# A gated MLP behind block attention on one core: the LayerNorm gain moved from v's rows to the gate, w_sg loaded in natural order, low parts last in batch 0, and a new order

## The chip, the cores and the metric

One core of a Trainium2 chip. Times are device microseconds (us) of one execution; a kernel's time is the median of its runs. Engines are named as the profile names them: PE (TensorE matmuls) and PEld (its weight loads), DVE (VectorE), ACT (ScalarE), POOL (GpSimd), SP (SyncE, which issues nearly all DMAs here).

## The reference, cut to what matters

Eight batches of 576 tokens, 8 heads of 64, all in float32. Attention works in chunks of 64 tokens; its output x (576 x 512 per batch) goes through a gated MLP:

```python
h = x @ w_in                                   # 512 -> 1024
h = 0.5 * h * (1.0 + np.tanh(c * (h + 0.044715 * h ** 3)))
u, v = (h[..., :d_ff // 2], h[..., d_ff // 2:])
mu = np.mean(v, axis=-1, keepdims=True)
var = np.mean((v - mu) ** 2, axis=-1, keepdims=True)
v_n = (v - mu) / np.sqrt(var + 1e-06) * g_ln   # g_ln: one number per feature (512)
v_s = np.einsum('ts,bsd->btd', w_sg, v_n) + b_sg[None, :, None]
gated = u * v_s
return (x + gated @ w_out).astype(np.float32)
```

Since g_ln does not depend on the token, it can be taken out of the sum over s: v_s = g_ln * (w_sg @ v' + b_sg / g_ln), with v' the normalised rows without the gain.

## The kernel before, in words

Every large product runs in pieces: an operand is split into a high part, rounded to the matmul's own format, and a low part (the rest), and three products (high by low, low by high, high by high) are summed in PSUM. `split` does this: ACT copies the high part, DVE subtracts it.

The MLP of a batch has four kinds of step: v units (`v_unit`, 128 tokens each, `m` 0 to 3; unit 4 holds the 64 odd tokens of two batches and runs in even batches only), u products (`u_unit`, `u_fast`), s units (`s_unit`, one per 128 features, which multiply w_sg with v's rows and gate with u) and o products. From batch 2 on (`FAST`) u and o use seven block products in place of eight, which needs sums of blocks (`x_sums`, `w_sums`). Each v unit ends in `normed`: gelu on ACT writes `hs`, DVE takes the statistics (`bn_stats`, `bn_aggr`, an addition), POOL raises to the power -1/2 (`sm<-sm,neg_half`), DVE forms (h - mean) * g (`hs<-hs,sm,g_bc`, with g_ln broadcast over 128 rows in `g_bc`), ACT multiplies by the power and rounds (`v<-hs,sm`), DVE forms the low part (`v<-hs,sm,v`). The bias b_sg enters `s_unit` as extra rows of the last product: rows 64 and 96 of `z2` hold ones, rows 64 and 96 of `wsg_l` the parts of b_sg.

Attention (`att_scores`, `att_transpose`, `att_out`) works on tiles of 128 tokens by 64x64 matmuls. Tiles 0 to 4 (`PE_TILES`) are transposed on PE through one PSUM tile `banks` (`banks<-ident,first_pts`), whose halves also take the tile's output; ACT and DVE carry that output to `xh`, `xl` and `xf`. The weights w_in arrive as 64-bit words; `W` and `w`, `X` and `x` turn them into `win_h`, `win_l` with the help of PE (`ident`, `lows`).

The order of all this is made in two stages. `START` (batches 0 and 1), `SLOTS`, `SUMS` and `ORDER` (batches 2 to 7) list steps: S scores, T transposes, O outputs of a tile, M the load of g_ln, G and g the load and split of w_sg, v, u, s, o as above, Y, V, J parts of weights and sums. Then `Plan` records all operations, and `emit` deals them out to the five engines with a price per operation (`Op.price`), due times counted back from PE's list, and `EARLY`, which shifts the due time of a step. Each engine then runs its list strictly in order. All instructions come out of one line of `emit`, so every row of the profile carries L266 (L271 after the change).

PSUM tiles `pm` and SBUF tiles of the pool `tmp` have four buffers each (`banks` holds one of the four in PSUM while tiles 0 to 4 run).

Of the kernel before, what the change touches and what calls it, by code (L numbers as in the profile page):

```python
# [12 lines left out]
F32 = mybir.dt.float32  # L13
F32R = mybir.dt.float32r
# [11 lines left out]
P = 128  # L26
# [8 lines left out]
LN_EPS = 1e-6  # L35
REST_ODD = ODD // 2
# [12 lines left out]
A0 L0 B0 A1 L1 L2 L3 B1 A2 A3 S0 W0 T0 S1 W1 S2 w0 w1 T1 W2 O0 O1 W3 w2 T2 S3 M0 w3 v00 O2 A4 T3 X0 O3 G0 S4 v01 A8  # L49
T4 O4 B8 x0 X1 v02 X2 x1 v03 X3 U1 v04 g0 x2 g3 x3 U0 g1 P5 F0 g2 u03 g4 u02 s00 P7 T5 F1 T6 s02 s01 Q5 s03 T7 T8 v10  # L50
Y6 Q7 v11 v12 Y3 u10 v13 Y2 u11 Y1 Y0 Y7 u13 Y5 u12 Y4 V0 A12 A10 o01 B10 V1 s10 A11 V2 P9 S13 s11 T9 s12 T10 o02 P11
s13 B11 T13 o00 Q9 T11 o03 A15 T12 o10 O13 V3 B15 B12 o11 Q11 J0 P14 J2 o13 A17 J1 o12
"""

SUMS = {(2, 13): "o3", (2, 8): "o0 o1", (2, 10): "o2"}
# [25 lines left out]
FAST_V = 8  # L81
ORDER = "u0 u1 u2 u3 u4 s0 s1 s2 s3 o0 o1 o2 o3"
# [9 lines left out]
EARLY = {'K*': 1, 'X*': -8, 's03': 2, 'Y0': -2, 'P7': 3, 'v04': -4, 'X0': -1, 'w3': -1, 'W*': -1, 'g4': 4, 'Y7': 2, 'A17': -2, 'x2': -2, 'A12': 1, 'F1': 0, 'B10': 4, 'o02': 2, 'u10': 1, 'T11': 0, 'v13': -1, 'B11': 4, 'u13': 5, 'B12': -2, 'u12': -2, 'u11': 2, 'x3': 2, 'J1': 3, 'P14': -7, 'J0': 0, 's02': -2, 'o10': 0, 'Q7': 4, 'g3': -1, 'Q11': 6, 'u02': 4, 'g0': 2, 'T10': -2, 'S13': -1, 'A10': 3, 'V1': -7, 'T13': -4, 'o01': -1, 'P9': 5, 'P5': -4, 'Q9': -2, 's00': 4, 'B15': 2, 'A11': 1, 'o13': 1, 'V0': -4, 'Q5': 4, 'g2': 8, 'T6': -2, 'Y6': 8, 'g1': -4, 'U0': -2}  # L92
# [44 lines left out]
class Op:  # L137
# [13 lines left out]
    def price(self):  # L151
# [4 lines left out]
        if self.engine == "tensor":  # L156
            x = ins[-1]
            n = outs[0].free_size()
            if x.dtype == F32R:
                return 2.5 + 0.45 * n, 190  # L160
            if x.dtype == BF16:
                return 4.6 + 0.42 * n, 190
            if ins[0].ap[0][1] == D:
                self.quarter = True
                return 29.5, 190
            return (109 if self.method == "transpose" else 1.83 * n + 10), 190
        if self.method == "dma_start" and self.engine == "gpsimd":
            return 1200, DMA_LATE + ins[0].size() / 100
        if self.method == "dma_start":
            row = ins[0].ap[-1][1]  # L170
            return (420 if row >= P else 620), DMA_LATE + ins[0].size() / row / 16 * (5 + 0.16 * row)
# [261 lines left out]
def block_attention_gated_mlp(ctx: ExitStack, tc: tile.TileContext, qkv, w_in, w_out, w_sg, g_ln, b_sg, out):  # L433
# [37 lines left out]
    g_bc = const.tile([P, DH], F32, name="g_bc")  # L471
# [221 lines left out]
    def load_w_sg():  # L693

        st = staged["s"] = [
            mp.tile([P, KT, S], F32, name="stage", tag="u2"),
            tmp.tile([P, S], F32, name="stage", tag="tmp"),
            tmp.tile([P, S], F32, name="bt", tag="tmp"),
        ]
        flat = lambda a: a.rearrange("p (j s) -> p j s", j=2)  # L700
        for j in range(2):
            src = w_sg[:, :4, j * REST_ODD : (j + 1) * REST_ODD]
            nc.sync.dma_start(out=st[0][:, :, j * HS : j * HS + REST_ODD], in_=src)
        for i in range(4):
            nc.sync.dma_start(out=flat(st[0][:, i, :])[:, :, REST_ODD:], in_=flat(w_sg[:, i, ODD:]))
        for dst, src in ((st[1], w_sg[:, 4, :]), (st[2][64:65], b_sg), (st[2][96:97], b_sg)):
            nc.sync.dma_start(out=flat(dst)[:, :, REST_ODD:], in_=flat(src[:, ODD:]))
            nc.sync.dma_start(out=flat(dst)[:, :, :REST_ODD], in_=flat(src[:, :ODD]))

    def split_w_sg(i):  # L710
        nonlocal wsg_h, wsg_l
        st, odd, bt = staged["s"]
        if i == 0:
            wsg_h, wsg_l = (w_sg_tile(i).rearrange("p (i s) -> p i s", i=5) for i in range(2))
            nc.gpsimd.memset(wsg_l[64:128, 4, :].bitcast(F32), 0.0)
        hi, lo = wsg_h[:, i, :], wsg_l[:, i, :]
        if i < 4:
            split(hi, lo, st[:, i, :], nc.scalar, nc.vector)
            return
        nc.scalar.copy(hi, odd)  # L720
        nc.vector.tensor_tensor(lo[0:ODD], odd[0:ODD], hi[0:ODD].bitcast(F32), op=ALU.subtract)

        nc.scalar.copy(lo[64:65], bt[64:65])
        bh = tmp.tile([P, S], F32R, name="bh", tag="tmp")
        nc.scalar.copy(bh[96:97], bt[96:97])
        nc.vector.tensor_tensor(lo[96:97], bt[96:97], bh[96:97].bitcast(F32), op=ALU.subtract)

    def load_misc():
        nc.sync.dma_start(out=g_bc, in_=g_ln.broadcast_to([P, DH]))
# [306 lines left out]
    def v_unit(b, m):  # L1036
# [7 lines left out]
        for kt in range(KT):  # L1044
# [18 lines left out]
    def normed(m, h):  # L1063
# [126 lines left out]
    def s_unit(b, dt):  # L1190
# [12 lines left out]
        nc.vector.tensor_tensor(row, pm[:, :, :HS], row, op=ALU.mult)  # L1203
# [261 lines left out]
```

## Time and profile before

| | us |
|---|---|
| median of 3 runs (lowest, highest) | 494.49 (494.19, 495.76) |
| the profiled execution, its time | 496.37 |
| its span (first to last instruction) | 494.3 |
| PE busy in the span | 473.2 (96%) |
| DVE busy | 400.8 (81%) |
| ACT busy | 335.5 (68%) |
| POOL busy | 126.7 (26%) |
| mean granted PE clock | 0.999 of full |

The busy time of PE counts a matmul from its start to its modelled end, and matmuls overlap, so how fast PE gets on is read from the distance between starts. PE's idle time and the waits behind it are in the list of waits, and the timeline shows at which instruction of a list an engine stood. Idle time of an engine that PE does not wait for costs nothing.

### The profile page before, as it was taken

How to read it: one execution, taken by the hardware profiler on the slowest of the kernel's cores; microseconds unless marked ns; L12 is line 12 of the kernel's file. 1: busy time of each engine (PE TensorE's matmuls, PEld its weight loads, DVE VectorE, ACT ScalarE, POOL GpSimd, SP SyncE). 2: the span in 40 equal slices, each digit the busy share in tenths (PEclk: the TensorE clock that was granted, in tenths of full speed). 3: DMA queues.
4: the chain of work that ended last, by engine and by line, in shares of the span. 5: the costliest groups of instructions: out<-in, count | busy, mean ns of one | idle time of the engine just before them, and what ended most of it. 6: DMA issues, size and time to landing. Idle time of an engine off the chain costs nothing.

```text
span 494.3 us, 12562 instructions
## 1 busy us (share of the span) xinstructions
PE 473.2 (96%) x5076; PEld 433.8 (88%) x5076; DVE 400.8 (81%) x712; ACT 335.5 (68%) x598; POOL 126.7 (26%) x115
## 2 busy tenths in 40 slices
PE   2989999999999999999999989999999999999995
PEld 1557899899999799989999779988999889998995
DVE  7898989887988886989779697888859796777275
ACT  4799698844596998538974698729985396844230
POOL 0105100053424338153203411062301612043000
PEclk9999999999999999999999999999999999999999
DMA  8897100244347525294435443376424703170303
GB/s 316 303 253 186 44 3 23 66 148 135 129 121 208 144 110 158 95 274 123 141 82 183 140 149 97 100 215 181 128 66 120 224 12 127 45 201 25 129 1 95
DMA packets 74746, 65.47 MB, mean 132 GB/s; under 512 B 46397, under 2 KB 59969, under 8 KB 74689
## 3 DMA queue, kind: packets, MB, share of 16 engines
q1 hardware_dynamic: 74416, 64.64, 43.3%
q8 instruction: 40, 0.66, 0.5%
q14 instruction: 18, 0.14, 0.1%
q10 hardware_dynamic: 272, 0.03, 0.0%
HBM read 52.07 MB, written 12.58 MB: 131 GB/s over the span
## 4 chain that ended last, share of the span: by engine, by line
PE 80%; ACT 7%; DVE 5%; DMA 4%; issue 2%; SPq 1%; DVEq 0%; ACTq 0%
PE pm L266 78%; DMA out_dram<-ot 2%; ACT ptT L266 2%; PE banks L266 2%; SPq L266 1%; DMA av<-qkv 1%; DVE nmax L266 1%; DVE ot L266 1%; DMA qk<-qkv 1%; ACT hs L266 1%; DVE wsg L266 1%; ACT v L266 1%; ACT third_pt L266 1%; ACT xf L266 0%; ACT ut L266 0%
## 5 line engine op out<-in xcount | busy, mean ns | idle before, releaser
L266 PE MATMUL pm<-wsg,v 128*128 128x288 f32 x768 | 110.2, 297 | 0.0
L266 PEld LDWEIGHTS pm<-wsg,v 128*128 128x128 f32 x768 | 104.1, 188 | 0.9
L266 ACT COPY ptT<-blocks 32x256 f32<-32x256 f32 (+1 forms) x140 | 62.7, 448 | 5.0 <-DVE blocks L266 1.9
L266 POOL TENSOR_TENSOR sm<-sm,neg_half 128x1 f32<-128x1 f32 x36 | 31.1, 865 | 111.2 <-DVE sm L266 94.4
L266 PE MATMUL pm<-gh,wout 128*128 128x288 f32 x272 | 54.6, 298 | 0.0
L266 PE MATMUL pm<-win_h,xl 128*128 128x512 f32 x128 | 51.5, 403 | 0.6 <-DVE xl L266 0.6
L266 PE MATMUL pm<-win_l,xh 128*128 128x512 f32 x128 | 50.7, 396 | 0.0
L266 PE MATMUL pm<-win_h,xh 128*128 128x512 f32 x128 | 50.5, 395 | 0.0
L266 ACT ACT_TABLE_LOAD x30 | 38.5, 1283 | 15.4 <-DVE pt L266 8.2
L266 PEld LDWEIGHTS pm<-gh,wout 128*128 128x128 f32 x272 | 42.7, 188 | 0.6
L266 POOL TENSOR_TENSOR pt<-pt,nmax 128x512 f32<-128x512 f32 x27 | 30.2, 1129 | 43.8 <-DVE nmax L266 39.7
L266 POOL TENSOR_TENSOR xs<-xf 128x576 f32<-128x576 f32 x12 | 17.2, 1434 | 92.0 <-ACT xf L266 81.2
L266 ACT CAST gh<-u 128x576 fp32r<-128x576 f32 x32 | 21.0, 672 | 27.5 <-DVE u L266 27.2
L266 DVE TENSOR_TENSOR u<-pm,u 128x576 f32<-128x576 f32 x32 | 24.1, 754 | 17.4 <-PE pm L266 16.9
L266 ACT CAST tx<-xs 128x576 fp32r<-128x576 f32 x24 | 16.1, 674 | 29.1 <-POOL xs L266 21.7
L266 PE MATMUL pm<-gl,wout 128*128 128x288 f32 x136 | 34.9, 295 | 0.0
L266 DVE TENSOR_TENSOR ot<-pm,xf 128x576 f32<-128x576 f32 x32 | 24.0, 752 | 10.1 <-PE pm L266 5.5
L266 DVE TENSOR_TENSOR gl<-u,gh 128x576 fp32r<-128x576 f32 x32 | 24.0, 753 | 9.9 <-ACT gh L266 9.8
L266 DVE BATCH_NORM_STATS2 sm<-hs 128x6 f32<-128x512 f32 x36 | 24.6, 685 | 8.7 <-ACT hs L266 8.7
L266 PEld LDWEIGHTS pm<-win_h,xl 128*128 128x128 f32 x128 | 24.0, 188 | 6.4 <-DVE xl L266 1.0
L266 DVE STREAM_TRANSPOSE blocks<-pt 128x512 f32<-128x512 f32 x31 | 21.8, 705 | 9.5 <-POOL pt L266 3.8
L266 PE MATMUL pm<-xh,win_l 128*128 128x288 f32 x112 | 28.5, 301 | 0.8 <-ACT hs L266 0.8
(161 smaller groups left out, 1172.5 us busy)
## 6 DMA issues: line engine op xcount, KB each, us to landing
qk<-qkv SPq DMA_DIRECT2D x31, 512.0 KB, 4.4
out_dram<-ot SPq DMA_DIRECT2D x32, 256.0 KB, 3.1
wx<-kept_u SPq DMA_DIRECT2D x30, 256.0 KB, 3.6
wx<-kept_o SPq DMA_DIRECT2D x30, 256.0 KB, 3.2
av<-qkv SPq DMA_DIRECT2D x116, 64.0 KB, 2.5
wsg<-w_in SPq DMA_DIRECT2D x4, 512.0 KB, 4.4
wout<-w_in SPq DMA_DIRECT2D x4, 512.0 KB, 7.8
st<-w_out SPq DMA_DIRECT2D x8, 256.0 KB, 2.8
```

The lines of the kernel that those rows point to most:

```text
L266: getattr(getattr(self.nc, op.engine), op.method)(*op.args, **op.kwargs)
```

## The change

Six things are changed together.

1. The gain. `normed` no longer multiplies by g_ln: one DVE operation subtracts the mean and multiplies by the power (it now needs POOL's result), ACT only copies the high part, DVE subtracts. `s_unit` multiplies by g_ln in the gate, as a number per partition (`g_col`). In `z2` the rows 64 and 65 hold the parts of 1/g_ln and row 96 its high part; `load_misc` forms them from a 2 KB load: ten small operations, four 128x128 transposes on PE, two copies on ACT. The six memsets of `z2` are gone.
2. w_sg and b_sg come in as they lie in memory (4 DMAs in place of 12) and are put into the order of tokens by `split_w_sg`, whose copies and subtractions go in two pieces each.
3. In batch 0 the products with `win_l` come last in each v unit (`LOW_LAST`).
4. `START`, `SUMS` and `SLOTS` list the steps in another order.
5. `EARLY` has other entries.
6. The prices in `Op.price` differ for DMAs, for 64x64 matmuls and for DVE operations with one wide operand.

```diff
 START = """
-A0 L0 B0 A1 L1 L2 L3 B1 A2 A3 S0 W0 T0 S1 W1 S2 w0 w1 T1 W2 O0 O1 W3 w2 T2 S3 M0 w3 v00 O2 A4 T3 X0 O3 G0 S4 v01 A8
...
+A0 L0 B0 A1 L1 L2 L3 B1 A2 A3 S0 W0 T0 S1 W1 S2 w0 w1 T1 W2 O0 O1 W3 w2 T2 S3 w3 v00 O2 A4 T3 X0 O3 G0 S4 v01 A8 T4
...
 SLOTS = {
-    6: "11:O56 9:T7 1:T5 14:T8 4:S78 14:O78 14:S9A 2:T6",
+    6: "9:T7 2:T5 13:T8 4:S78 14:O78 14:S9A 11:O56 4:T6",
...
+LOW_LAST = (0,)
...
-    for z in z2:
-        zf = z.bitcast(F32)
-        nc.vector.memset(zf[64:128, :], 0.0)
-        nc.vector.memset(zf[64:65, :], 1.0)
-        nc.vector.memset(zf[96:97, :], 1.0)
...
-        for j in range(2):
-            src = w_sg[:, :4, j * REST_ODD : (j + 1) * REST_ODD]
-            nc.sync.dma_start(out=st[0][:, :, j * HS : j * HS + REST_ODD], in_=src)
...
+        for dst, src in (
+            (st[0], w_sg[:, :4, :]), (st[1], w_sg[:, 4, :]), (st[2][64:66], b_sg.broadcast_to([2, S])), (st[2][96:97], b_sg)
+        ):
+            nc.sync.dma_start(out=dst, in_=src)
...
+        by_halves(nc.scalar.copy, hi, src)
+        minus = lambda a, x, y: nc.vector.tensor_tensor(a, x, y.bitcast(F32), op=ALU.subtract)
+        by_halves(minus, lo[:n], src[:n], hi[:n])
...
     def load_misc():
-        nc.sync.dma_start(out=g_bc, in_=g_ln.broadcast_to([P, DH]))
+        nc.sync.dma_start(out=g_col, in_=g_ln.rearrange("o (k p) -> p (o k)", p=P))
...
+        for k in range(KT):
+            nc.tensor.transpose(ps[:, k * P : (k + 1) * P], rows[:, k, :], ident)
+        for z in z2:
+            nc.scalar.copy(z[64:128, :], ps[64:128, :])
...
+        if b in LOW_LAST:
+            steps.sort(key=lambda x: x[1].tensor.name == win_l.tensor.name)
...
-        nc.vector.scalar_tensor_tensor(h, h, mv[:, 0:1], g_bc, op0=ALU.subtract, op1=ALU.mult)
+        nc.vector.tensor_scalar(h, h, mv[:, 0:1], rs, op0=ALU.subtract, op1=ALU.mult)
...
-            nc.scalar.mul(hi, h, rs)
-            nc.vector.scalar_tensor_tensor(lo, h, rs, hi.bitcast(F32), op0=ALU.mult, op1=ALU.subtract)
+            split(hi, lo, h, nc.scalar, nc.vector)
...
-        nc.vector.tensor_tensor(row, pm[:, :, :HS], row, op=ALU.mult)
+        nc.vector.scalar_tensor_tensor(row, pm[:, :, :HS], g_col[:, dt : dt + 1], row, op0=ALU.mult, op1=ALU.mult)
```

Three places show how the engines' lists move. The first is PE's list from the second tile's transposes to the first v unit (`pm<-win_h,xl`). In the rows, `banks<-...first_ptT` are outputs of a tile, `pm<-qkv_w` and `pm<-qkv_u` scores of tiles 2 and 4 and of tile 3, `ident` and `lows` the weights' conversion. Before:

```order
L266 MATMUL pm<-win_l,ident 128x512
L266 MATMUL banks<-first_ptT,av 64x64 x16
L266 MATMUL pm<-qkv_w 64x64 x16
L266 MATMUL pm<-wsg_97,ident 128x512
...
L266 MATMUL banks<-ident,third_pt 128x128 x4
L266 MATMUL pm<-win_h,xl 128x512
...
L266 MATMUL pm<-win_l,xh 128x512
L266 MATMUL pm<-win_h,xh 128x512
...
L266 MATMUL banks<-first_ptT,qkv_w 64x64 x16
L266 MATMUL pm<-qkv_w 64x64 x16
L266 MATMUL pm<-wsg_110,ident 128x512
```

After:

```order
L271 MATMUL pm<-qkv_w 64x64 x16
L271 MATMUL banks<-first_ptT,av 64x64
L271 MATMUL pm<-win_l,ident 128x512
L271 MATMUL pm<-wsg_97,ident 128x512
L271 MATMUL banks<-first_ptT,av 64x64
...
L271 MATMUL pm<-qkv_w 64x64 x16
L271 MATMUL banks<-ident,third_pt 128x128 x4
L271 MATMUL pm<-win_h,xl 128x512
L271 MATMUL pm<-win_h,xh 128x512
...
L271 MATMUL pm<-win_l,xh 128x512 x4
L271 MATMUL banks<-first_ptT,qkv_w 64x64 x16
L271 MATMUL pm<-wsg_110,ident 128x512
```

Scores of tiles 2, 3 and 4 moved ahead, the outputs of tile 0 and the scores of tile 3 are now cut up by conversions, and the four products with `win_l` stand at the end of the unit.

The second is ACT's list in the v units of batch 6 (`hs<-pm` is the gelu that empties a v unit's PSUM tile; `z` and `v` are high parts, `ptT<-blocks` a tile's transposed probabilities). Before:

```order
L266 ACT_TABLE_LOAD
L266 ACTIVATE hs<-pm 128x512 x2
L266 CAST tx_572<-xs 128x576
L266 ACTIVATE v<-hs,sm 128x512
L266 COPY ptT<-blocks 128x512
L266 COPY ptT<-blocks 32x8x32
L266 ACTIVATE hs<-pm 128x512
L266 COPY ptT<-blocks 32x8x32 x3
L266 ACTIVATE hs<-pm 128x512
...
L266 COPY ptT<-blocks 32x8x32
L266 ACTIVATE hs<-pm 128x512
```

After:

```order
L271 ACT_TABLE_LOAD
L271 ACTIVATE hs<-pm 128x512 x2
L271 COPY xf<-xf_ident 128x4x32
L271 COPY xf<-xf_lows 128x4x32
L271 ACTIVATE hs<-pm 128x512
...
L271 COPY ptT<-blocks 32x8x32 x2
L271 ACTIVATE hs<-pm 128x512
L271 CAST v<-hs 128x512
L271 COPY ptT<-blocks 32x8x32 x2
L271 ACTIVATE hs<-pm 128x512
```

The third gelu now stands ahead of the first high parts, and the fourth and fifth follow sooner.

The third is DVE's list at the end of the v units of batch 7. Before:

```order
L266 TENSOR_SCALAR sm<-sm 128x1
L266 SCALAR_TENSOR_TENSOR v<-hs,sm,v 128x512
L266 SCALAR_TENSOR_TENSOR hs<-hs,sm,g_bc 128x512
L266 BN_STATS sm<-hs 128x6
L266 SCALAR_TENSOR_TENSOR v<-hs,sm,v 128x512
L266 BN_AGGR sm<-sm 128x2
L266 TENSOR_SCALAR sm<-sm 128x1
L266 SCALAR_TENSOR_TENSOR hs<-hs,sm,g_bc 128x512
L266 SCALAR_TENSOR_TENSOR v<-hs,sm,v 128x512
```

After:

```order
L271 TENSOR_SCALAR hs<-hs,sm 128x512
L271 BN_STATS sm<-hs 128x6
L271 BN_AGGR sm<-sm 128x2
L271 TENSOR_TENSOR v<-hs,v 128x512
L271 TENSOR_SCALAR sm<-sm 128x1
L271 TENSOR_SCALAR hs<-hs,sm 128x512
L271 TENSOR_TENSOR ut<-pm,ut 128x576
L271 TENSOR_TENSOR v<-hs,v 128x512
```

The wide operation on `hs` stood directly behind the addition before, where POOL's power ran beside it; it now needs that power, and in this last unit it still stands directly behind the addition.

## Rows read from the trace of the kernel before

**Rows 1.** The page: span, and the busy line of its part 1.
```profile
span 494.3 us, 12562 instructions
...
PE 473.2 (96%) x5076; PEld 433.8 (88%) x5076; DVE 400.8 (81%) x712; ACT 335.5 (68%) x598; POOL 126.7 (26%) x115
```

**Rows 2.** Waits of PE: us in total, times, longest.
```profile
PE pm L266 <- DMA qk<-qkv: 7.2, 2, 4.3
PE pm L266 <- ACT hs L266: 2.3, 2, 1.5
PE banks L266 <- ACT first_pts L266: 2.3, 1, 2.3
PE banks L266 <- DVE xl L266: 1.3, 1, 1.3
PE pm L266 <- ACT ut L266: 0.7, 2, 0.5
...
PE pm L266 <- DVE xl L266: 0.6, 1, 0.6
```

**Rows 3.** Timeline of PE, 34 to 38: start, us, instruction, [idle before].
```profile
34.76 0.66 PE L266 MATMUL banks<-ident,first_pts 128*128 128x128 f32 x4 [1.29 <-DVE xl L266]
35.17 0.48 PE L266 MATMUL pm<-win_h,xl 128*128 128x512 f32 x1
...
35.95 0.39 PE L266 MATMUL pm<-win_h,xl 128*128 128x512 f32 x1
36.27 1.15 PE L266 MATMUL banks<-first_ptT,qkv_u 64*64 64x64 f32 x32
37.35 0.51 PE L266 MATMUL pm<-win_l,xh 128*128 128x512 f32 x1
37.69 0.40 PE L266 MATMUL pm<-win_h,xh 128*128 128x512 f32 x1
37.93 0.40 PE L266 MATMUL pm<-win_h,xl 128*128 128x512 f32 x1
```

**Rows 4.** Timeline of ACT at 30.
```profile
30.18 1.28 ACT L266 ACT_TABLE_LOAD   x1
```

**Rows 5.** Timeline of ACT in batch 6, 397 to 403.
```profile
397.25 0.60 ACT L266 ACTIVATE hs<-pm 128x512 f32<-128x512 f32 x1 [0.22 <-DVE v L266]
...
399.13 0.60 ACT L266 ACTIVATE hs<-pm 128x512 f32<-128x512 f32 x1
...
402.94 0.60 ACT L266 ACTIVATE hs<-pm 128x512 f32<-128x512 f32 x1
```

**Rows 6.** Groups on DVE: out<-in, shapes, count, then busy us, mean ns, idle before.
```profile
L266 DVE SCALAR_TENSOR_TENSOR hs<-hs,sm,g_bc 128x512 f32<-128x512 f32 x36 | 27.6, 773 | 0.0
L266 DVE TENSOR_TENSOR u<-pm,u 128x576 f32<-128x576 f32 x32 | 24.1, 754 | 17.4 <-PE pm L266 16.9 <-ACT u L266 0.4
L266 DVE SCALAR_TENSOR_TENSOR v<-hs,sm,v 128x512 fp32r<-128x512 f32 x32 | 23.8, 749 | 4.4 <-ACT v L266 4.1
...
L266 DVE TENSOR_TENSOR pt<-pt,nmax 128x512 f32<-128x512 f32 x4 | 2.6, 679 | 0.1
...
L266 DVE TENSOR_SCALAR wsg<-wsg 128x512 f32<-128x512 f32 x4 | 1.7, 417 | 0.0
```

**Rows 7.** Groups on ACT: the high part with and without a factor.
```profile
L266 ACT ACTIVATE v<-hs,sm 128x512 fp32r<-128x512 f32 x32 | 22.9, 723 | 7.4 <-POOL sm L266 3.1 <-DVE hs L266 2.9 <-DVE sm L266 1.1
...
L266 ACT CAST wx<-r 128x512 fp32r<-128x512 f32 x6 | 3.4, 619 | 1.9 <-DVE wout L266 1.8
```

**Rows 8.** Groups on POOL.
```profile
L266 POOL TENSOR_TENSOR sm<-sm,neg_half 128x1 f32<-128x1 f32 x36 | 31.1, 865 | 111.2 <-DVE sm L266 94.4 <-ACT wout L266 8.4 <-ACT hs L266 3.6
...
L266 POOL TENSOR_TENSOR xs<-xf,xs 128x576 f32<-128x576 f32 x12 | 19.5, 1629 | 29.2 <-DVE tx L266 28.1 <-DVE nmax L266 1.1
```

**Rows 9.** Timelines of DVE and POOL at 13: two operations beside each other.
```profile
13.37 1.53 DVE L266 TENSOR_TENSOR win_l<-wsg,win_h 128x512 fp32r<-128x512 f32 x1
...
13.05 1.30 POOL L266 TENSOR_TENSOR first_pts<-first_pts,nmax 128x512 f32<-128x512 f32 x1 [11.74 <-DVE nmax L266]
```

More of the change, by code (lines that the diff above doesn't have):

```diff
@@ L35 @@
 LN_EPS = 1e-6
+G_TINY, G_TOP = 1e-30, 3.0e38
 REST_ODD = ODD // 2
@@ L170, in price @@
             row = ins[0].ap[-1][1]
-            return (420 if row >= P else 620), DMA_LATE + ins[0].size() / row / 16 * (5 + 0.16 * row)
+            each = 15 + 0.22 * min(max(row - 64, 0), 192) + 0.09 * max(row - 256, 0)
+            return (420 if row >= P else 620), DMA_LATE + ins[0].size() / row / 16 * each
         wide = [a for a in ins if a.free_size() > 1]
@@ L186, in price @@
                 return (170 if self.method == "reciprocal" else 100 if self.method == "bn_aggr" else 70), 85
-            one = len(ins) == 1 and not psum and self.method in ("tensor_copy", "tensor_scalar")
+            one = len(wide) == 1 and not psum and self.method in ("tensor_copy", "tensor_scalar")
             three = self.method == "scalar_tensor_tensor" and not psum and len(ins) > 2
@@ L470, in block_attention_gated_mlp @@
     win_l = const.tile([P, KT, DF], F32R, name="win_l")
-    g_bc = const.tile([P, DH], F32, name="g_bc")
+    g_col = const.tile([P, KT], F32, name="g_col")
     neg_half = const.tile([P, 1], F32, name="neg_half")
@@ L716, in split_w_sg @@
         hi, lo = wsg_h[:, i, :], wsg_l[:, i, :]
+        src, n = (st[:, i, :], P) if i < 4 else (odd, ODD)
+        by_halves(nc.scalar.copy, hi, src)
+        minus = lambda a, x, y: nc.vector.tensor_tensor(a, x, y.bitcast(F32), op=ALU.subtract)
+        by_halves(minus, lo[:n], src[:n], hi[:n])
         if i < 4:
-            split(hi, lo, st[:, i, :], nc.scalar, nc.vector)
             return
-        nc.scalar.copy(hi, odd)
-        nc.vector.tensor_tensor(lo[0:ODD], odd[0:ODD], hi[0:ODD].bitcast(F32), op=ALU.subtract)
-        nc.scalar.copy(lo[64:65], bt[64:65])
+        by_halves(nc.scalar.copy, lo[64:66], bt[64:66])
         bh = tmp.tile([P, S], F32R, name="bh", tag="tmp")
-        nc.scalar.copy(bh[96:97], bt[96:97])
-        nc.vector.tensor_tensor(lo[96:97], bt[96:97], bh[96:97].bitcast(F32), op=ALU.subtract)
+        by_halves(nc.scalar.copy, bh[96:97], bt[96:97])
+        by_halves(minus, lo[96:97], bt[96:97], bh[96:97])
     def load_misc():
-        nc.sync.dma_start(out=g_bc, in_=g_ln.broadcast_to([P, DH]))
+        nc.sync.dma_start(out=g_col, in_=g_ln.rearrange("o (k p) -> p (o k)", p=P))
+        gain = tmp.tile([P, S], F32, name="gain", tag="tmp")
+        rows = gain[:, : 4 * P].rearrange("p (k c) -> p k c", k=KT)
+        part = [gain[:, 4 * P + i * KT : 4 * P + (i + 1) * KT] for i in range(3)]
+        nc.gpsimd.memset(gain, 0.0)
+        nc.scalar.activation(part[0], g_col, AF.Abs)
+        nc.vector.tensor_scalar(part[0], part[0], G_TINY, G_TOP, op0=ALU.max, op1=ALU.min)
+        bits = g_col.bitcast(I32)
+        nc.vector.scalar_tensor_tensor(
+            bits, bits, -0x80000000, part[0].bitcast(I32), op0=ALU.bitwise_and, op1=ALU.bitwise_or
+        )
+        nc.vector.reciprocal(part[0], g_col)
+        hi = part[1].bitcast(F32R)
+        split(hi, part[2], part[0], nc.scalar, nc.vector)
+        for at, src in ((64, part[1]), (65, part[2]), (96, part[1])):
+            nc.vector.tensor_copy(rows[:, :, at : at + 1], src.unsqueeze(2))
+        ps = ps_m.tile([P, 2, 512], F32, name="pm")[:, 0]
+        for k in range(KT):
+            nc.tensor.transpose(ps[:, k * P : (k + 1) * P], rows[:, k, :], ident)
+        for z in z2:
+            nc.scalar.copy(z[64:128, :], ps[64:128, :])
     wout_h = wout_l = wsg_h = wsg_l = None
```

26 lines of the change are left out of this document (11 added, 15 removed), and 8 rows, old and new, of the table SLOTS.

## The prediction

> **What bounds the kernel now.** I read the page first: PE is busy in 473.2 of a span of 494.3 us, DVE in 400.8, ACT in 335.5 [rows 1]. So PE sets the end, and what can be won is its idle time, 494.3 - 473.2 = 21.1 us. The list of PE's waits says what that is made of [rows 2]: 7.2 us for the first tiles' data, which the change does not touch (the first 11 DMAs stand in the same order); 2.3 for the second tile's softmax; then 1.3 and 0.6 on the low parts `xl`, 2.3 on gelus of v units, 0.7 on copies `ut`. The waits behind the first two tiles add up to 1.3 + 0.6 + 2.3 + 0.7 = 4.9 us; most of the rest is the empty end behind the last matmul, whose list is the same after the change. Whatever DVE and ACT save, the kernel gains at most about 5 us, and only where one of these waits ends sooner. The timeline then shows where two of them sit: PE stands 1.29 us before the transposes of tile 3 at 34.76 [rows 3], and in batch 6 the fifth gelu of the v units comes 3.8 us behind the fourth (402.94 against 399.13) [rows 5].
>
> **The change, part by part.**
>
> *Off DVE and ACT.* The wide operation on `hs` takes 773 ns 36 times [rows 6]. It becomes a `TENSOR_SCALAR` with two operands per partition. No row has that form; the nearest one, the same operation on 128x512 floats with constants, takes 417 ns, and the ceiling is that nothing changes, 773. I take 417, since only the source of the two numbers differs: 36 x 0.356 = 12.8 us of DVE. The Trainium skill, "VectorE: DVE Perf Modes", section "Mode 2×_2P — use both read ports for one tensor", says that an operation with one tensor of float32 in SBUF can deliver two elements per cycle and one with two tensors cannot; by it the 417 would hold, and were it void here the saving would be 0. The low part goes from 749 to a subtraction as at 679: 32 x 0.07 = 2.2 us off. The gate has a third operand now; 754 is the floor, and I put the same 0.07 on top, 32 x 0.07 = 2.2 us added. DVE loses about 13 us net. On ACT the high part falls from 723 to 619 ns [rows 7], 3.3 us over 32, and its list has 28 table loads in place of 30, each 1.28 us [rows 4]. None of this is on PE's path by itself.
>
> *On PE, added.* Four transposes for 1/g_ln. Four like them took from 34.76 to 35.17, 0.41 us [rows 3]; they stand between u products in a stretch where PE doesn't wait: +0.4 us. Their PSUM tile is held until two copies on ACT are done, and I cost that at nothing, since some forty u products follow them in the list; without that cover it is two copies at 0.62.
>
> *On PE, detours.* Going from large to 64x64 matmuls and back costs time: 36.27 - 35.95 = 0.32 us into one, and 37.69 - 37.35 = 0.34 behind it, against 0.24 between neighbours (37.93 - 37.69) [rows 3], so about 0.2 us for a round trip. I counted 75 changes of size in PE's list before and 85 after: five more round trips. One of them stands late, +0.2. Four stand in the first 35 us, where PE partly waits anyway: 0 to +0.8, I take +0.4.
>
> *The early stage.* The scores of tile 4 come before v00, so ACT does both exponentials ahead of one table load instead of loading three times between 30 and 40 us. This takes two loads, 2.56 us, from ACT where it is nearly full. The low parts last in v00 let it start without `win_l` of the last block. Against it: tile 3's transposes now have only one conversion between them and tile 2's output, where before the scores of tile 4 stood there too, and they still need the `xl` that DVE forms from that output behind a statistics operation. So the 1.29 us can shrink or grow. Ends: all of it goes (-1.3, and -1.1 more if half of the 2.3 of the second tile went too) or nothing does (0). I take -0.9, nearer to the first end, since the two table loads that go are worth twice the wait.
>
> *The late waits.* In batch 6 the third gelu moves ahead of the first high parts and the others follow it; the five gelus lose about four operations of 0.6 us ahead of the last one. The shorter of the two gelu waits, 2.3 - 1.5 = 0.8 us [rows 2], goes: -0.8. The longer, in batch 4, has the same gelus behind the same neighbours, each 0.1 shorter; it begins with a store that lands late, which stays: -0.3 of 1.5. The `ut` waits (0.7) lie behind high parts and table loads that get shorter or go: -0.4. The `xl` wait in batch 1 has one shorter copy ahead of it: -0.2 of 0.6.
>
> *DMAs.* SP issues 8 fewer, and one broadcast of 256 KB gives way to a load of 2 KB in single elements. No row has such a load. It stands before the loads of two u weight blocks, which wait for their buffers anyway; I take 0, between a gain of half a microsecond and a loss of one.
>
> **Sum:** 0.4 + 0.2 + 0.4 - 0.9 - 0.8 - 0.3 - 0.4 - 0.2 = -1.6 us, against the profiled execution's 496.37 (span 494.3 and 2.07 around it): 494.8. That execution lies 1.9 above the median of the runs; carried to the median of 494.49 it gives **492.9 us**, faster by 0.32%. About 0.3%, 1.5 us, is what a measurement of this kernel can tell from no change (its own three runs span 0.3%), so the forecast lies just beyond that line.
>
> **The rivals.**
>
> *The waits move, nothing is won.* DVE has no slack in the first 50 us, and its list puts the softmax of tile 4 ahead of the `xl` of tile 2's output. Then tile 3's transposes wait as long as before while conversions that stood ahead of them are still to do: the early -0.9 becomes +0.3. Of the late waits only batch 6's goes, -0.8. With 0.4 + 0.2 + 0.4 this gives +0.5: 495.0, no measurable change. For it: PE's list shows two conversions behind the transposes that stood ahead before. Against it: ACT's two table loads.
>
> *DVE stands at the gain.* In `normed` the wide operation needs POOL's power now, where it ran beside it before. The power takes 865 ns, and an `xs` ahead of it on POOL 1629 [rows 8]. DVE runs in order, so behind a waiting `hs` stand the low parts and the additions to `ut` that free PSUM. A second way to the same: DVE and POOL hinder each other. At 13 us a subtraction took 1.53 us beside a POOL multiplication of 1.30 [rows 9], against 0.68 for its kind [rows 6]. The Trainium skill, "SBUF — State Buffer", section "Who interferes with whom", speaks of a port pair that one of the two holds for a whole instruction, the fast one-tensor operation included; the trace agrees for two-tensor operations, with the 1.53. It decides if DVE stands more than the 0.43 us per unit that it saves; per batch of four units a microsecond each is 4 - 1.7 = 2.3 us late. If in each of the six batches from the third on PE then waits once more for the 0.5 us of the longest `ut` wait [rows 2], that is +3.0, with 1.0 added and the early -0.9: 494.49 + 3.1 = 497.6, slower. Against it: DVE's list mostly has two to four other operations between the addition and `hs` (only the last unit of batch 7 has none), and PE has 72 u products to do before it needs v.
>
> *All waits go.* With DVE 13 us lighter, the 4.9 us vanish and only 0.6 (transposes and the late round trip) is added: 490.2.
>
> **How the numbers follow.** Forecast as summed, with small errors either way, faster: 0.40; all waits gone or nearly so: 0.12; together faster 0.52. No measurable change: 0.34. DVE stands at the gain, slower: 0.14. The range reaches from the third case, with the other 1.1 us of the early bound, 490.2 - 1.1 = 489.1, up to 494.49 + 1.4 = 495.9, where nothing is won and all is added (0.4 + 0.2 + 0.8). The slow rival lies outside, 0.14. The forecast's own range is 491.0 to 493.0.
>
> **What would show it.** Right: 36 `TENSOR_SCALAR` on `hs` near 0.42 us, DVE at about 388 us busy, PE's wait on `banks` for `xl` under 0.7, one gelu wait left in PE's list, near 1.2 us, and PE idle in about 20 us or less. The early term is wrong if the first products with `wsg` and v's rows start no sooner than before. The slow rival shows as DVE waiting for `sm` from POOL, some microseconds per batch, with PE waiting for `ut` or for v's low parts. If DVE and ACT are lighter as said, PE's waits are as long as before and the time stays, the second case holds.

## The result, and the profile after

The changed kernel takes 498.48 us (median of 6 runs, 496.58 to 498.9), the kernel before 494.5 in the same set: a ratio of 1.0068, 95% interval 1.0048 to 1.0088. A second set, with more runs of before, gives 498.44 against 495.61, 1.0050 (1.0036 to 1.0063). So it is slower, by the ratios 2.5 to 3.4 us, where 1.6 us less was forecast.

Its profiled execution is the fastest of its eleven (496.58); the page therefore looks like that of before [rows 1], span and busy PE alike:

```profile
span 494.4 us, 12537 instructions
...
PE 472.9 (96%) x5076; PEld 433.3 (88%) x5080; DVE 395.4 (80%) x719; ACT 331.1 (67%) x607; POOL 119.8 (24%) x116
...
L271 POOL TENSOR_TENSOR sm<-sm,neg_half 128x1 f32<-128x1 f32 x36 | 24.3, 674 | 104.3 <-DVE sm L271 104.2
...
L271 ACT ACT_TABLE_LOAD x28 | 35.9, 1283 | 8.6 <-DVE pt L271 4.0
```

DVE is 5.4 us lighter, not 13; ACT has its two table loads less. The groups that answer to rows 6 and 7 (DVE, then ACT; count, then busy us, mean ns, idle before):

```profile
L271 DVE SCALAR_TENSOR_TENSOR u<-pm,g_col,u 128x576 f32<-128x576 f32 x32 | 26.0, 813 | 19.7 <-PE pm L271 19.5
L271 DVE TENSOR_TENSOR v<-hs,v 128x512 fp32r<-128x512 f32 x32 | 23.2, 730 | 2.8 <-ACT v L271 2.5
L271 DVE TENSOR_SCALAR hs<-hs,sm 128x512 f32<-128x512 f32 x36 | 19.4, 540 | 0.9 <-POOL sm L271 0.7
...
L271 ACT CAST v<-hs 128x512 fp32r<-128x512 f32 x32 | 19.6, 619 | 7.2 <-DVE hs L271 6.8
```

The operation on `hs` takes 540 ns, between the 417 I took and the 773 of before; the last column answers the slow rival, since DVE stood for POOL's power only 0.7 us in all. All 36 took 498 to 550 ns, with POOL at work beside them or not, so POOL is not what lengthens them; of the 36 of before, one that ran beside POOL's multiplication `r` took 1.78 us, and the mean of the others is 744. The Trainium skill, "VectorE: DVE Perf Modes", section "Mode 2×_2P — use both read ports for one tensor", makes the one-tensor form the faster one: the 540 against 773 agrees in direction, but the form with two operands per partition did not reach the 417 of the form with constants.

The list of PE's waits is where the change shows [rows 2]:

```profile
PE pm L271 <- DMA qk<-qkv: 7.3, 3, 4.3
PE banks L271 <- ACT first_pts L271: 2.6, 1, 2.6
PE banks L271 <- DVE xl L271: 1.3, 2, 0.8
PE pm L271 <- DVE wsg L271: 0.8, 1, 0.8
PE pm L271 <- ACT first_ptT L271: 0.6, 1, 0.6
PE pm L271 <- ACT ut L271: 0.6, 2, 0.4
PE pm L271 <- DVE gain L271: 0.5, 1, 0.5
PE pm L271 <- DMA av<-qkv: 0.5, 2, 0.3
PE pm L271 <- DVE ot L271: 0.5, 1, 0.5
PE pm L271 <- DVE xl L271: 0.5, 1, 0.5
PE pm L271 <- DVE ut L271: 0.4, 1, 0.4
```

The gelus (`hs`, 2.3 before) are gone from it, both of them, where the prediction had one left near 1.2. In their place stand shorter waits that before did not have: for `wsg` (ahead of a conversion at 32.64), `gain`, `av`, `ot`, for DVE's `ut`, and a second place on `xl`. (The 0.6 for `first_ptT` is no new one: it lies at 13.5, where before waits 0.6 for `wsg`.)

To see where the time went in every trace, I cut PE's timeline at five products that all kernels have: A ends at the first product of the third v unit, B at batch 1's first v unit, C at the 137th `pm<-gh,wout` (in batch 2), D and E at the first v unit of batches 4 and 5, F at the last `pm<-gh,wout`. "rise" is the time at which the trace's record of TensorE's clock begins, at 2.4 GHz.

```
kernel          rise     A      B      C      D      E      F    falls of the clock
before          18.96  39.91  43.25  121.37  67.47  53.06  157.30
before_again    17.93  39.61  43.25  121.40  68.28  50.87  157.96
before_again2   19.33  39.85  43.25  121.40  68.08  52.63  157.34
changed         16.49  40.19  44.37  123.03  68.29  50.63  155.91
a_again         19.87  41.76  44.39  123.69  68.32  50.45  156.05
b_gain          18.75  39.50  44.93  122.09  68.69  52.03  157.30
b_newprice      17.08  41.59  44.04  121.98  68.46  52.28  156.46
b_neworder2     19.80  39.91  43.93  123.08  70.14  53.96  159.67   at 300
b_listprice     18.48  42.21  43.89  122.95  69.88  51.89  156.64
a_oldorder      17.25  40.49  44.95  122.01  67.98  50.61  156.64
a_oldprice      17.94  39.60  48.04  121.64  69.31  52.41  158.23   at 62
a_rowgain       18.30  41.06  43.92  124.43  68.68  50.96  156.56
o_rowgain       19.39  41.72  44.53  121.87  68.74  50.59  157.32
a_early         19.57  44.08  44.37  123.31  68.31  50.47  156.58   at 37
a_early_row     18.56  44.87  44.44  123.53  68.97  51.17  156.14   at 36
o_early         19.64  44.09  44.09  122.19  67.95  50.70  156.12   at 37
o_early_row     20.01  44.05  45.74  122.37  68.04  50.68  156.30   at 37
a_early24       19.02  41.41  44.39  122.92  68.30  50.07  156.42
a_early42       19.19  40.06  46.17  123.23  68.39  50.13  156.02
o_early24       17.25  40.69  44.08  122.31  68.34  50.33  156.95
```

The changed kernel (two traces) against before (three): A +0.3 to +2.2, B +1.1, C +1.6 to +2.3, E -0.2 to -2.6, F -1.3 to -2.1. It loses in about the first 210 us (A to C) what it wins in batches 4 to 7, and more.

### The profile page after: what moved, and what is told of

Read it like the earlier page. It is cut to its first block, busy times and chain, and to the rows that moved or that the text cites. A ratio compares the mean times of both kernels' runs of the same rounds, so it can differ in the third digit from the quotient of the medians.

```text
span 494.4 us, 12537 instructions
## 1 busy us (share of the span) xinstructions
PE 472.9 (96%) x5076; PEld 433.3 (88%) x5080; DVE 395.4 (80%) x719; ACT 331.1 (67%) x607; POOL 119.8 (24%) x116
## 4 chain that ended last, share of the span: by engine, by line
PE 63%; DVE 13%; ACT 10%; DMA 7%; SPq 3%; issue 2%; ACTq 0%; DVEq 0%
PE pm L271 62%; SPq L271 3%; ACT ptT L271 3%; DMA qk<-qkv 2%; DMA out_dram<-ot 2%; DVE sm L271 2%; DMA wout<-w_in 2%; ACT L271 1%; DVE ot L271 1%; DVE v L271 1%; DMA av<-qkv 1%; DVE nmax L271 1%; DVE xl L271 1%; PE banks L271 1%; ACT hs L271 1%
## 5 line engine op out<-in xcount | busy, mean ns | idle before, releaser
L271 POOL TENSOR_TENSOR sm<-sm,neg_half 128x1 f32<-128x1 f32 x36 | 24.3, 674 | 104.3 <-DVE sm L271 104.2
L271 PE MATMUL pm<-win_l,xh 128*128 128x512 f32 x128 | 48.4, 394 | 0.0
L271 DVE SCALAR_TENSOR_TENSOR u<-pm,g_col,u 128x576 f32<-128x576 f32 x32 | 26.0, 813 | 19.7 <-PE pm L271 19.5
L271 DVE TENSOR_REDUCE nmax<-pm 128x16 f32<-128x1024 f32 (+1 forms) x22 | 22.5, 1022 | 9.3 <-PE pm L271 9.2
L271 PEld LDWEIGHTS pm<-win_h,xh 128*128 128x128 f32 x128 | 24.0, 188 | 5.2
L271 PEld LDWEIGHTS pm<-win_l,xh 128*128 128x128 f32 x128 | 24.0, 188 | 5.1
```

The costliest lines, as they stand in the source:

```text
L271: getattr(getattr(self.nc, op.engine), op.method)(*op.args, **op.kwargs)
```

## The experiments

Each ratio is to the kernel before, on the same chip in the same set, with its 95% interval; medians of before by set are 495.61, 494.67, 496.39, 495.34 and 496.13.

**The changed kernel again, and before twice more.** No edit.

> The changed kernel, unaltered, a second time. Its profiled execution had a span of 494.4 us, five other executions 496.1 to 496.8, and the kernel before has 494.3 in its profile but a median of 494.5 in time, so the trace at hand is not the usual case. Theory A (the loss lies in a stage whose timing varies from execution to execution): the new trace has a span near 496.3, and beside the first one it shows 2 us more in one place, most likely in the first 50 us. Theory B (every execution of the changed kernel carries the loss in the same waits, and only the first trace was lucky): the time is 498.5 again, and the 2 us are spread over many waits of 0.3 to 0.8 us. Expected: median 498.0 to 498.9.

Measured: 498.44 us. The new trace (span 496.7) is 1.57 us behind the first one at the end of A and 0.66 in C, and nowhere else by more than 0.2. So both theories hold in part: most of the spread comes from the first 20 us (PE's rows are 1.57 us apart from there to 40 us, one by one), the rest from waits in batch 2.

> The kernel before, unaltered, a second time. Its profiled execution (496.37) lies above the median of its runs (494.5 to 495.6 in three sets). Theory luck (the waits that the prediction meant to remove, 1.7 us at 286 and 0.95 at 402, belong to that execution and are the 1.9 us by which it exceeds the median): this trace has a span of 492 to 493.5 and lacks one or both waits. Rival (they stand in every execution, and the spread comes from the moment at which the clock rises): both waits are there again within 0.2 us, and the 40-us milestone moves with the rise by 0.46 us per us, as it does between five traces of the changed early order.

> The same once more, for a third trace: of three, theory luck expects the two waits in one or at most two; the rival expects them in all.

Measured: 495.72 (0.9984, 0.9968 to 0.9999: the same kernel twice, so 0.16% is what chance does) and 496.54 in one run. The wait for gelus in PE's list is 2.3 us in the first trace [rows 2], 2.0 in the third, but 0.7 in the second, whose E is 50.87: the wait in batch 4 stands in two of three, that of batch 6 in all. So 1.5 of the 2.3 us that the prediction saw there stand in two executions of three, and not in the third. Stage A hardly moves with the rise here.

**Parts of the change, each alone or left out.** Names with a_ are made from the changed kernel, with b_ from the kernel before, with o_ from the changed kernel with the lists of before. b_gain is before with the gain at the gate; b_newprice with the three prices; b_neworder2 with the four lists (M0, the load of g_ln, stays where before has it, since there the first v unit still needs g_bc); b_listprice with both; a_oldorder and a_oldprice are the changed kernel with the lists, or the prices, of before. For example:

```diff
-            return (420 if row >= P else 620), DMA_LATE + ins[0].size() / row / 16 * (5 + 0.16 * row)
+            each = 15 + 0.22 * min(max(row - 64, 0), 192) + 0.09 * max(row - 256, 0)
+            return (420 if row >= P else 620), DMA_LATE + ins[0].size() / row / 16 * each
```

> The changed kernel with the four lists of the kernel before; only M0 stands where the changed kernel has it, before g0. Theory order: 493 to 495, since DVE and ACT are lighter and the old lists have their few waits. Theory gain: 497.5 to 498.5, as the changed kernel. If lists and edits only work together: above 499.

> The kernel before with the gain moved to the gate and 1/g_ln in z2 (M0 before g0), its own lists, prices, load of w_sg and order of products in batch 0. Theory order: 493 to 495. Theory gain: 497 to 498.5, and the trace shows PE waiting for gain (0.5 us) and, in most batches, for v's low parts or for ut.

> The changed kernel with the three prices of the kernel before; lists, gain, w_sg and order of products as changed. PE's list up to the first v unit is again that of the kernel before. Theory early (the new prices pulled scores and conversions of weights ahead, to where a matmul still takes twice as long, and cost about 1.4 us by 40 us): the milestone at 40 us (first product of the third v unit) stands 1 to 1.5 us sooner than in the changed kernel at the same moment of the clock's rise, and the time is 496.5 to 497.5. Rival (the early stage differs only by the moment at which the clock rises, which is chance): 498.4 as the changed kernel.

> The kernel before with the changed kernel's three prices and nothing else. Its PE list up to the first v unit is that of the changed kernel. Theory early: slower than before by 1 to 2 us, 496.5 to 497.5. Rival (chance of the clock alone): 495 to 496, no change.

> The kernel before with the changed kernel's four lists alone (M0, the load of the gain, stays where the kernel before has it). Theory order (the new lists put PE in front of sums, copies and outputs that are late in batches 2 and 3): 497 to 499, with new waits of 0.5 to 0.9 us on ut and ot between 150 and 270 us, and without the 1.7 us wait at 286. Theory gain and early only: 494 to 495.5, since in the changed kernel's trace batches 4 and 6 gain 3.7 us against the trace of before.

> The kernel before with both the changed kernel's lists and its prices, but with its own gain in v's rows, load of w_sg and order of products. Lists alone gave +1.6%, prices alone +0.7%. Theory fit (lists and prices belong together and were each useless alone): within 0.3% of before or faster, 493.5 to 496. Theory sum (each costs by itself): +2% or more, above 502. Between them (496.5 to 500): the lists fit the gain at the gate too.

Measured:

| kernel | us | ratio |
|---|---|---|
| a_oldorder | 496.42 | 1.0015 (1.0002 to 1.0028) |
| b_gain | 499.80 | 1.0085 (1.0068 to 1.0103) |
| b_newprice | 498.59 | 1.0073 (1.0053 to 1.0093) |
| b_neworder2 | 502.21 | 1.0159 (1.0132 to 1.0186) |
| b_listprice | 502.15 | 1.0122 (1.0099 to 1.0145) |
| a_oldprice | 503.73 | 1.0169 (1.0143 to 1.0195) |

No theory explains this alone, and the parts do not add up. Each costs 0.7 to 1.6% by itself, lists and prices together 1.2% where their sum is 2.3%, and the whole 0.5 to 0.7%. One can be left out with profit, the lists: a_oldorder takes 496.42, the changed kernel in the same set 498.44, 1.0015 (1.0002 to 1.0028) against 1.0050 (1.0036 to 1.0063), two intervals that do not meet. So with gain and prices in place the new lists cost 2.0 us, and the 0.15% that is left is hardly more than chance. That a part alone leaves the planner with lists tuned for something else would fit the other results, but no run shows it. The load of w_sg and the low parts last are in every a_ and o_ kernel and were never run alone, so what they are worth is open.

The stages tell the parts apart. *Prices*: PE's rows up to the first product of the first v unit go with the prices (the kernels with the new ones share one order there, those with the old ones another), and A goes with them: 39.5 to 39.9 with the old, 40.2 to 42.2 with the new. b_newprice and b_listprice, which lack the low parts last, lie 1.1 us above the line of the changed kernel's A against the rise (given below); this fits a gain by the low parts. *Gain*: B is 43.25 before, 43.9 to 44.0 in the kernels that changed only lists or prices, and 44.4 to 45.0 with the transposes (48.0 in a_oldprice is taken up below), so 0.6 to 0.8 of the growth needs no transposes. b_gain shows in small what its theory asked for: a wait of 0.48 for `gain`, and in each of batches 2 to 6 one of 0.27 to 0.63 for `ut` or v's low parts. *Lists*: C is 121.4 to 122.1 with the old lists, 123.0 to 123.7 with the new ones in four traces of five (a_oldprice has 121.6). *Batch 4*: but for one execution of before, an E of 51 or less came only with gain and new prices together (b_gain 52.0, b_newprice 52.3, b_listprice 51.9).

Two of these kernels show something more. In a_oldprice the clock fell. PE's timeline there, and behind it the busy time by stretch (us, PE busy, granted clock, DMA share, GB/s):

```profile
60.37 0.63 PE L270 MATMUL pm<-ident,gain 128*128 128x128 f32 x4 [0.98 <-DVE gain L270]
62.15 0.73 PE L270 MATMUL pm<-xh,win_l 128*128 128x288 f32 x2 [1.15 <-ACT z L270]
62.68 0.68 PE L270 MATMUL pm<-xl,win_h 128*128 128x288 f32 x2
63.16 0.68 PE L270 MATMUL pm<-xh,win_h 128*128 128x288 f32 x2
```

```profile
58.00:62.00 4.00, 2.02 (x71) 1.00 0.41 131
62.00:66.00 4.00, 3.85 (x17) 0.57 0.00 0
66.00:70.00 4.00, 4.00 (x33) 1.00 0.02 4
```

After waits of 0.98 and 1.15 us, with 64 products of 64x64 ahead of the first and four transposes between them, the granted clock is 0.57 over four microseconds, the level of 1.2 GHz for most of them, and a pair of products advances by 0.48 us (62.68 to 63.16), against 0.26 to 0.27 in the changed kernel's timeline at 61. In b_neworder2 one wait of 2.08 us did the same:

```profile
298.20 0.40 PE L266 MATMUL pm<-xh,wx 128*128 128x288 f32 x1 [2.08 <-ACT ut L266]
```

So a wait of two microseconds can cost more than its own length. It need not: o_early_row (below) waits 2.32 us at 75.44, and the clock stays up.

```profile
74.00:78.00 4.00, 2.56 (x74) 1.00 0.02 3
78.00:82.00 4.00, 4.00 (x33) 1.00 0.01 4
```

The Trainium skill, "TensorE: Matmul & The Clock Gate", section "HAM oscillation — how this bites in real kernels", names idle gaps of PE as what lets the clock fall, and longer ones than these. The traces agree in the kind and not in the length: 2.08 us was enough in one execution, 2.32 was not in another.

**1/g_ln without PE.** a_rowgain writes the parts to DRAM and reads them back as rows; o_rowgain is the same with the lists of before.

```diff
-        for k in range(KT):
-            nc.tensor.transpose(ps[:, k * P : (k + 1) * P], rows[:, k, :], ident)
-        for z in z2:
-            nc.scalar.copy(z[64:128, :], ps[64:128, :])
+        for i in range(2):
+            nc.sync.dma_start(out=rows[i : i + 1, :].rearrange("o (k p) -> p (o k)", p=P), in_=part[1 + i])
+        for z in z2:
+            nc.sync.dma_start(out=z[64:66, :].bitcast(F32), in_=rows)
+            nc.sync.dma_start(out=z[96:97, :].bitcast(F32), in_=rows[0:1, :])
```

> The changed kernel with 1/g_ln brought into z2's rows by DMA (parts written to DRAM, read back as rows) in place of four transposes on PE, and M0 moved ahead of w3. Theory gain on PE: the transposes and PE's wait for them cost 1.1 us (a step of 0.93 us before them, 0.43 for them), so the milestone at 83 us stands 1.0 to 1.3 us sooner and the time is 497.0 to 497.5. Rival (the stretch up to 83 us is bound by DVE and ACT, and PE waits elsewhere as long): 498.0 to 498.9.

> The changed kernel with the four lists of before, M0 where before has it, and 1/g_ln brought into z2's rows by DMA instead of four transposes. With the old lists and the transposes it was 1.0015 of before, with 1.4 us of PE's time lost ahead of the transposes and 0.43 in them. Theory gain on PE: 1.0 to 1.7 us less than that, 0.997 to 0.999 of before, which beats both kernels. Rival (any edit of the plan shifts waits elsewhere by a us or more): 1.001 to 1.008.

Measured: 499.88 (1.0095, 1.0074 to 1.0117) and 498.49 (1.0050, 1.0033 to 1.0068). B is 43.92 and 44.53, so 0.4 to 0.5 us come back there, and nothing of it reaches the end: both are slower than the kernels that they were made from. o_rowgain lies in the range of its rival; a_rowgain lies above the ranges of its theory and of its rival (which ended at 498.9), with PE waiting elsewhere: 1.05 for `xl` at 93.48, where the changed kernel waits 0.48, and a C of 124.43.

**The first 30 us alone, the rest kept row by row.** The planner deals the operations out twice, the second time with the DMA price of before; whatever starts before the cut in the second plan comes first, in that order. a_early cuts at 30 us, o_early does so with the lists of before; the `_row` kernels also leave out the transposes.

```diff
+        at2 = None
+        for _ in range(3):
+            at2 = self.run(users, after, at2)
+        at = [b - 1e6 if b < FIRST else a for a, b in zip(at, at2)]
```

> The changed kernel, its order behind the first v unit kept instruction by instruction; only the first 30 us are dealt out with the DMA price of before, so that the four conversions of weights stand again behind the 64x64 products. Theory early: the 40-us milestone stands at -0.4 to 0 us against the first trace of before, whatever the moment of the clock's rise (the changed kernel: +0.3 to +1.85, 0.46 us per us of later rise), and the gain is kept to the end: 1.0 to 1.4 us under the changed kernel, a ratio of 1.002 to 1.004. Rival (what is won early is lost at the next wait on DVE, as with the transposes): ratio 1.005 to 1.007 as before.

> As a_early, and the four transposes and two copies for 1/g_ln taken out of the lists (six DMAs bring the rows to z2), everything else in its place. Theory: PE gets on 0.7 to 1.1 us further by 83 us, ratio 1.000 to 1.002. Rival: PE waits for xl at 91 us that much longer, ratio as a_early.

> The changed kernel with the four lists of before (1.0015 of before), and the first 30 us as in a_early, everything else in its place. Theory: 1.0 to 1.4 us under that, ratio 0.9985 to 0.9997. Rival: 1.0015 again.

> As o_early, without the transposes and copies for 1/g_ln. Theory: 0.7 to 1.5 us less than o_early, ratio 0.9955 to 0.998, which beats both kernels. Rival: as o_early.

Measured: 500.41 (1.0100, 1.0077 to 1.0122), 501.91 (1.0121, 1.0092 to 1.0149), 498.90 (1.0069, 1.0048 to 1.0090) and 501.99 (1.0151, 1.0116 to 1.0185). All miss. The cut itself made a wait, and the clock fell behind it (a_early):

```profile
35.20 1.12 PE L280 MATMUL pm<-wsg,ident 128*128 128x512 f32 x2 [3.20 <-DVE wsg L280]
```

The rows by DMA came too late for the first products with `z`; o_early_row stood there for 2.32 us:

```profile
75.44 0.76 PE L286 MATMUL pm<-wsg,z 128*128 128x288 f32 x4 [2.32 <-DMA z<-rows]
```

**The cut moved to 24 and to 42 us.**

> As a_early, with the cut at 24 us instead of 30: a_early stood 3.4 us at 31.5, where the work of the two pieces met badly, and its clock fell to 1.2 GHz behind that wait. PE's first 30 rows are those of before, the other engines' lists differ from the changed kernel's in 15 to 19 rows. Theory early: the first product of the first v unit stands within 0.5 us of before's (the changed kernel: +1.2 to +2.8), the 40-us milestone at 0 to +0.5 whatever the rise, and the time 0.5 to 1.4 us under the changed kernel, ratio 1.002 to 1.005. Rival (the wait ahead of the weights' conversion at 32 us takes it all): the 40-us milestone at +1 or more, ratio 1.005 to 1.007.

> The same with the cut at 42 us: the whole early stage, tile 3 and the first three v units in the order that the old DMA price gives. Theory early: 40-us milestone at -0.4 to 0, ratio 1.001 to 1.004, unless a new wait of about 0.8 us at the cut (42 us) or ahead of the transposes for 1/g_ln takes part of it. Rival: ratio 1.005 or more.

> The changed kernel with the four lists of before (1.0015) and the cut at 24 us. Theory early: ratio 0.9985 to 1.0005. Rival: 1.0015 or more.

Measured: 497.83 (1.0031, 1.0022 to 1.0041), 498.38 (1.0044, 1.0030 to 1.0058) and 496.48 (1.0012, 0.9998 to 1.0026). With the cut at 24 PE's rows are those of before up to 25.25 in a_early24 (25.14 in before), and still the first product of v comes at 28.92 (before: 26.46) and A is that of the changed order at the same rise (41.41, and 40.69 in o_early24). So what A loses is dealt out behind these rows: the milestone came as the rival said, though the time of a_early24 lies in the theory's range. Why a_early24 is 0.2 to 0.4% better than the changed kernel stays open (they ran in different sets). With the cut at 42 the early stage is back (A 40.06, 1.35 us less than in a_early24 at about the same rise), but B is 46.17: new waits of 0.65 and 0.57 us, and PE reaches batch 1 at 86.23 (A and B together), where a_again, with a rise 0.7 us later, was at 86.15.

```profile
45.63 2.13 PE L280 MATMUL pm<-win_h,xodd 128*128 128x512 f32 x8 [0.65 <-ACT xodd L280]
56.62 0.54 PE L280 MATMUL pm<-xh,win_l 128*128 128x288 f32 x2 [0.57 <-ACT hs L280]
```

What A wins, B gives back. That ACT and DVE hold PE in this stage whatever its own order fits the two waits, but no run takes their work away, so it is argued and not shown. No version here beats the kernel before; a_oldorder and o_early24 come nearest.

## Why the prediction was wrong, step by step

The prediction added up the waits that before already has, and put at nothing those that the new order would make. Two places of its sum failed by that: the early stage, and batches 1 and 2 (C), where it expected about nothing.

**The early stage** (-0.9, with +0.4 for detours). This step failed. It was priced from ACT's table loads; the loads did go, but A is longer by 0.3 to 2.2 us, and the first products with `wsg` and v's rows start at 68.25 against 65.69, the prediction's own sign that this term is wrong. The wait of 1.29 ahead of tile 3's transposes [rows 3] did not shrink but was divided in three, 2.2 us together. PE, changed kernel:

```profile
27.32 0.63 PE L271 MATMUL banks<-ident,third_pt 128*128 128x128 f32 x4 [0.58 <-DVE xl L271]
...
32.64 1.13 PE L271 MATMUL pm<-wsg,ident 128*128 128x512 f32 x2 [0.84 <-DVE wsg L271]
...
34.52 0.66 PE L271 MATMUL banks<-ident,first_pts 128*128 128x128 f32 x4 [0.75 <-DVE xl L271]
```

The two cuts show where this comes from. a_early24 has the same three waits (0.55, 0.84, 0.75); a_early42, which keeps the order of before up to 42 us, has one of 1.50 and ends A 1.35 us sooner, 0.6 of it by shorter waits. So that much is lost by what is dealt out between 24 and 42 us. PE in a_early24, and below it in a_early42:

```profile
19.05 1.12 PE L280 MATMUL pm<-wsg,ident 128*128 128x512 f32 x2
...
25.25 1.12 PE L280 MATMUL pm<-wout,ident 128*128 128x512 f32 x2 [0.47 <-ACT win_l L280]
...
28.53 0.63 PE L280 MATMUL banks<-ident,third_pt 128*128 128x128 f32 x4 [0.55 <-DVE xl L280]
```

```profile
26.23 0.60 PE L280 MATMUL banks<-ident,third_pt 128*128 128x128 f32 x4
```

In a_early24 32 scores of tile 4 and a conversion now stand ahead of tile 2's transposes, and DVE does a maximum and a subtraction of tile 3's softmax before it forms the `xl` that they need. DVE in a_early24, then in before:

```profile
27.71 0.68 DVE L280 TENSOR_TENSOR xl<-banks,xh 128x512 fp32r<-128x512 f32 x1
```

```profile
24.83 0.68 DVE L266 TENSOR_TENSOR xl<-banks,xh 128x512 fp32r<-128x512 f32 x1
```

How long A is in one execution depends also on when the clock rises. The new prices moved conversions of weights ahead of the outputs of tile 0 (in a_early the old DMA price alone put the rows back). When the rise is late they fall before it, at 1.2 GHz, and they are PE's longest matmuls. PE in a_again, whose clock rose at 19.87, and in before, where the same pair comes behind the outputs:

```profile
16.81 0.79 PE L271 MATMUL pm<-win_l,ident 128*128 128x512 f32 x1
17.40 1.91 PE L271 MATMUL pm<-wsg,ident 128*128 128x512 f32 x2
```

```profile
18.95 1.13 PE L266 MATMUL pm<-wsg,ident 128*128 128x512 f32 x2
...
26.11 0.60 PE L266 MATMUL banks<-ident,third_pt 128*128 128x128 f32 x4
```

In the first trace of the changed kernel (rise at 16.49) the pair takes 1.02, and the waits are the same as in a_again; so the clock makes the spread between the two, and not the three waits. In five traces of kernels with the same early rows A goes from 40.19 (rise at 16.49) over 40.49 (17.25), 41.06 (18.30) and 41.72 (19.39) to 41.76 (19.87): 1.57 / 3.38 = 0.46 us per us. a_early24 and o_early24, with the old rows at first, give 0.41 per us (41.41 at 19.02, 40.69 at 17.25). The kernels with the old rows throughout have A between 39.50 and 39.91, but their rises all lie between 17.93 and 19.80. The prediction never asked at which level of the clock these matmuls would stand.

**The transposes** (+0.4, "in a stretch where PE doesn't wait"). Mis-sized: between 0.45 us, by which B is shorter without them (a_rowgain against the changed kernel), and the 0.9 of their rows. They take 0.38, but PE waited 0.53 ahead of them, a wait that the change itself brought. The rest of B's +1.1 is not theirs: kernels that changed only lists or prices have 0.6 to 0.8 of it. PE, changed kernel:

```profile
60.40 0.63 PE L271 MATMUL pm<-ident,gain 128*128 128x128 f32 x4 [0.53 <-DVE gain L271]
60.78 0.38 PE L271 MATMUL pm<-xh,win_l 128*128 128x288 f32 x1
```

I costed what the new operations put on PE and not when their operands are ready: the small operations that form the rows end on DVE at 60.24, behind work that was there first:

```profile
59.94 0.30 DVE L271 COPY gain<-gain 128x4 f32<-128x4 f32 x3
```

**The `ut` waits** (-0.4). Wrong sign. The old one of 0.47 at 296 us fell only to 0.36 and 0.27 (a_again), and new ones came. No wait stands between 150 and 190 us in the trace of before; the changed kernel has three, and a_again the same three, up to 0.68:

```profile
152.52 0.68 PE L271 MATMUL pm<-ptT,av 64*64 64x64 f32 x26 [0.34 <-DMA av<-qkv]
183.00 1.86 PE L271 MATMUL pm<-tx,wx 128*128 128x288 f32 x12 [0.25 <-ACT ut L271]
186.38 0.40 PE L271 MATMUL pm<-tx,win_l 128*128 128x288 f32 x1 [0.44 <-DVE ut L271]
```

With the old lists (a_oldorder) none of the three is there, so they need the new lists; with the lists alone (b_neworder2) only the first is, so the lists alone do not make them. This is the step that failed worst, C at +1.6 to +2.3: the prediction compared lists only at places where before waits, and never where the new lists make PE wait anew. All waits in C add up to 1.51 us (2.07 in a_again) against 0.56 before, which is 0.95 of the first trace's 1.66; the rest is PE getting on more slowly without a wait, of which one more change to 64x64 and back, the +0.2 of the sum, is a part.

**The late waits** (-0.8 and -0.3). Right in place and sign, too small. F falls by 1.3 to 2.1 and E by 0.2 to 2.6; the upper ends are executions of before that had the wait in batch 4. The new order of steps was not needed for it: with the lists of before (a_oldorder) the gelu waits are gone too, and E is 50.61. The `xl` wait in batch 1 fell by 0.1 (0.56 to 0.48), not by 0.2.

**DVE** (13 us off). It lost 5.4. On `hs` 36 x (540 - 417) = 4.4 us did not come, and about 1 us of the saving forecast there was the single operation of 1.78 us; the low part takes 730 on average and not 679. Since the ceiling was 5 us of waits, this decided little.

**The rivals.** "The waits move" was the right kind, down to DVE's softmax ahead of an `xl`, at +0.5 where the runs show +2.5 or more. "DVE stands at the gain", which carried the chance of slower, did not happen: 0.7 us in all, with two to four operations between. So slower came true by a way that had no chance of its own.

**Carrying to the median.** Sum and trace were one execution each. Of the changed kernel the traced one was its fastest, of before a slow one. Their mean spans (494.1 of three, 495.55 of two) differ by 1.5 us, the medians of the runs by 2.8 to 4.0; the rest lies in executions without a trace and stays open.

## What to carry to other kernels

Where a planner deals out the work, a price or a list is part of the kernel: judge such a change by looking for new waits along the whole of the bound engine's list, not only by the old waits that it removes. Take a wait as something to win only if it stands in more than one execution. When an edit adds work to the bound engine, ask when its operands are ready; the wait ahead of it can cost more than the work.

## What the runs showed of the hardware

TensorE's clock rose between 16.5 and 20.0 us into executions whose first matmuls were alike. Until then the columns of the stretches show a granted clock of 1.00, because the record begins with the rise; only durations tell (1.91 against 1.13 for the same pair). It also fell in the middle of a run, at 62 us behind two waits of 0.98 and 1.15 us and at 300 behind one of 2.08 (and at 36 to 37, with the cut at 30 us, behind one of 3.20); at 75 in another kernel one of 2.32 did not let it fall. A one-tensor DVE operation with two operands per partition took 540 ns on average (498 to 550, with POOL busy beside it or not), with constants 417. Two such operations of other kernels were longer: 1007 ns beside POOL's memset of `gain` in b_gain, 1209 beside POOL's `r` in a_oldorder.
